# One product of the first batch on GpSimd, and a later load of w1, in a spectral filter followed by a low-rank mixer

## The chip, the cores and the metric

The kernel runs on one core of a Trainium2 chip. The metric is the device time of one execution in microseconds. Before the change the median of three runs is 516.92 us (514.62 to 517.74).

## What is computed

x has 8 batches of 3136 x 256 values in f32. Each batch goes through a real Fourier transform along the 3136, a multiplication by a complex filter per frequency and column, and the transform back. The result y then goes through a low-rank mixer along the 3136 and a two-layer network along the 256:

```
X = rfft(x, axis=1);  y = irfft(X * (filt_r + 1j * filt_i), n=3136, axis=1)
h = y.transpose(0, 2, 1) @ U @ V            # U: 3136 x 32, V: 32 x 3136
u = y + h.transpose(0, 2, 1)
out = u + relu(u @ w_ch1) @ w_ch2           # w_ch1: 256 x 1024, w_ch2: 1024 x 256
```

## The kernel before, in words

The transform of length 3136 is split as 49 x 64. For each batch `f1` or, for batches 0 and 1, `f1_turned` (L269) does the first stage on TensorE. `mid` (L319) does the middle: it goes over 12 pairs of frequency groups k = (1, 2), (3, 4) ... (23, 24) and the single group k = 0, which comes third. In this text pairs are counted from 0, so pair 9 is k = (19, 20); with k = 0 in the third place it is step i = 10 of the loop. For each step a first product `pz` on TensorE (L384), then a multiplication of `pz`, read from PSUM, with both parts of the filter `fab` on VectorE (L392), which gives `uv`; then, some steps later, `s3` (L334): a second product `pe` on TensorE (L345, in batch 0 two matmuls, and an unread one ahead of it that keeps TensorE busy), which ScalarE copies to `e3` (L355). How many steps later is set by the length that the list `todo` may have (L398).

The results are turned in DRAM. SyncE's queue stores `e3` in groups of two pairs to `ct` (L364; of the third group, pairs 8 and 9 together and pair 10 alone), and `load_e2` (L412) loads each group back, turned, as rows of `eb` (L416). Pair 11 of batch 0 goes straight to `eb` as four single rows, two on SyncE's queue and two on GpSimd's (L359). Instructions of one queue leave in order, so a store that stands behind a load back waits until that load's own stores have landed. `rank` (L419) multiplies `e3` with the transformed U (`uh`), which gives h; VectorE copies h to the first 32 rows of `eb` (L438). `s4` (L445) multiplies `eb` with `sv`, whose first 32 rows are V, reordered from `vnat` by `v_rows` (L200); its result is `ut`, that is u. `mm1` (L484) and `mm2` (L538) are the two layers, over groups of 512 rows.

For batches 1 to 7 a plan deals the steps of the other stages between the `mm1` and `mm2` of earlier rows. For batch 0 the order is written out by hand (L580 to L625), and that is where the change lies:

- GpSimd's queue issues the loads of the filters, V (`vnat`), `sv`, the first x of batch 1 and w1 (L593), then copies the third part of the filters to the upper 64 partitions in four copies (`spread_filters(2)`, L160), then reorders the first half of V (L595), and later issues its two rows of pair 11.
- The 13 steps of `mid` follow; after step 8 ScalarE copies `uh` out of PSUM (`u_copied`, L236, two copies), after step 10 the load back of group 0 is put into SyncE's queue. Then come a further part of `mid`, the load back of group 1, the first 20 matmuls of `rank`, the rest of `mid` with its loads back, the second half of V on VectorE, and the rest of `rank`.
- Then GpSimd reads a few values of `eb` into `seen` (L620), which makes it wait until the loads back have landed; behind that it issues the further x loads of batch 1 and the load of w2 (L623).

PSUM banks of `pz` come from a ring of four (`z`), those of `pe` in batch 0 from a ring of two (`o`). The pool tag `asb` has four buffers that batch 0 does not use.

Of the kernel before, what the change touches and what calls it, by code (L numbers as in the profile page):

```python
# [11 lines left out]
F32 = mybir.dt.float32  # L12
# [4 lines left out]
NQ, NR = 49, 64  # L17
# [13 lines left out]
def row_of(k1, part):  # L31

    return 4 * (2 * ((k1 - 1) % 8) + part) + (k1 - 1) // 8
# [47 lines left out]
def kernel(  # L81
# [11 lines left out]
    nc = tc.nc  # L93
# [15 lines left out]
    sb = ctx.enter_context(tc.tile_pool(name="sb", bufs=1))  # L109
    ps = ctx.enter_context(tc.tile_pool(name="ps", bufs=2, space=bass.MemoryType.PSUM))  # L110

    def bank(tag, name, dtype=F32):

        return ps.tile([128, 512 if dtype == F32 else 1024], dtype, tag=tag, bufs=4 if tag == "z" else 2, name=name)

    def dram(t, off, dims):
        return bass.AP(tensor=t, offset=off, ap=[list(d) for d in dims])

    def view(t, off, dims):
        return bass.AP(tensor=t.tensor, offset=t.offset + off, ap=[[t.ap[0][0], t.shape[0]]] + [list(d) for d in dims])  # L120
# [39 lines left out]
    def spread_filters(i):  # L160
        s = slice(PARTS[i], PARTS[i + 1])
        copies = ((nc.vector.tensor_copy, nc.scalar.copy), (nc.vector.tensor_copy, nc.scalar.copy),
                  (nc.gpsimd.tensor_copy, nc.gpsimd.tensor_copy))[i]

        for s in (slice(PARTS[2], 19), slice(19, NK)) if i == 2 else (s,):
            for f, copy in enumerate(copies):
                copy(fab[64:128, f, s, :], fab[0:64, f, s, :])
# [12 lines left out]
    w1sb = cst.tile([128, 2, NH], F16)  # L180
# [19 lines left out]
    def v_rows(copy, a, z):  # L200
        copy(sv[0:RANK, a:z], vnat.rearrange("p (q r) -> p r q", r=NR)[:, a:z])
# [60 lines left out]
    def unread(p, n, size=512):  # L262
        for _ in range(n):
            nc.tensor.matmul(p[:, 512 - size:512], m64[:, 0:128], m64[:, 0:size], start=True, stop=True, skip_group_check=True)
# [29 lines left out]
    def turn(b, g):  # L294
        if g == 3:
            t = a20[b]
            pt = bank("z" if b else "o", "pt", F16)
            for dh in range(2):
                nc.tensor.transpose(pt[0:64, 128 * dh:128 * dh + 128], t1[b][1][:, dh, :], idn)
            nc.scalar.copy(t[0:64], pt[0:64, 0:DM])  # L300
            return t
        t = sb.tile([128, 8, DM], F16, tag="a2", bufs=3, name="a2")
        for half in range(2):
            pt = bank("m" if b == 0 and g == 1 and half == 0 else "z", "pt", F16)
            if b == g == half == 0:
                unread(pt.bitcast(F32), 2)
            for i in range(4):
                for dh in range(2):
                    nc.tensor.transpose(pt[:, 256 * i + 128 * dh:256 * i + 128 * dh + 128],
                                        t1[b][0][:, dh, 8 * g + 4 * half + i, :], idn)  # L310
            (nc.scalar.copy if half or (g and b == 0) else nc.vector.tensor_copy)(  # L311
                t[:, 4 * half:4 * half + 4, :].rearrange("p k d -> p (k d)"), pt)
        return t
# [5 lines left out]
    def mid(b, tag="z"):  # L319
        a2 = {}  # L320

        def load_a2(g):
            if b < 2:
                a2[g] = turn(b, g)
                return
            if g == 3:
                t = a20[b % 2]
                nc.sync.dma_start(t[0:64], ct0[b].ap())
            else:
                t = sb.tile([128, 8, DM], F16, tag="a2", bufs=3, name="a2")  # L330
                nc.sync.dma_start(t, dram(ct1[b], 8 * g * DM, [[24 * DM, 128], [1, 8 * DM]]))
            a2[g] = t

        def s3(ks, uv, o):  # L334
            n = len(ks) * DM
            i = (ks[0] - 1) // 2
            pe = bank(tag, "pe")

            direct = b == 0 and ks[0] > 22
            ms = (gmp, gsmp) if direct or not ks[0] else (gm, gsm)  # L340
            if b == 0 and ks[0] > 8:

                unread(pe, 1)
            for f, w in enumerate(ms if b == 0 else ms[:1]):
                nc.tensor.matmul(pe[:, 0:n], w, uv[:, f, o:o + n], start=(f == 0), stop=(b > 0 or f == 1))  # L345
            if not ks[0]:
                e3[b, 6] = sb.tile([128, DM], F16, tag="e30", bufs=2, name="e30")
                nc.scalar.copy(e3[b, 6], pe[:, 0:n])

                nc.sync.dma_start(eb[96:97, :, :], e3[b, 6][0:64])  # L350
                return
            if i % 2 == 0:
                e3[b, i // 2] = sb.tile([128, 4, DM], F16, tag="e3", bufs=6, name="e3")
            t = e3[b, i // 2]
            nc.scalar.copy(t[:, 2 * (i % 2):2 * (i % 2) + 2, :].rearrange("p k d -> p (k d)"), pe)  # L355
            if direct:
                for n, k in enumerate(ks):
                    for part in range(2):
                        (nc.sync if part else nc.gpsimd).dma_start(  # L359
                            eb[32 + row_of(k, part):33 + row_of(k, part), :, :],  # L360
                            t[64 * part:64 * part + 64, 2 * (i % 2) + n, :])
            elif i % 2 or b == 0 and i == 10:
                n = 4 if i % 2 else 2
                nc.sync.dma_start(dram(ct2[b][i // 4], 2 * (i % 4 // 2 * 2) * 128 * DM, [[DM, 128], [128 * DM, n], [1, DM]]), t[:, 0:n, :])  # L364

        if b == 0:
            spread_filters(0)
        for g in (0, 3, 1, 2) if b > 1 else (0, 3):
            load_a2(g)
        todo = []  # L370
        first_at = 2 if b < 2 else 6
        for i, ks in enumerate(PAIRS[:first_at] + [(0,)] + PAIRS[first_at:]):
            n = len(ks) * DM
            if b == 0 and i == 1:
                spread_filters(1)
            if b < 2 and i in (3, 7):
                load_a2(i // 4 + 1)
            pz = bank("z", "pz")
            if b == i == 0:
                unread(pz, 2)  # L380
            if ks[0]:
                src = a2[(ks[0] - 1) // 8]
                k = (ks[0] - 1) % 8
                nc.tensor.matmul(pz, a2m, src[:, k:k + 2, :].rearrange("p k d -> p (k d)"), start=True, stop=True)  # L384
            else:
                nc.tensor.matmul(pz[:, 0:n], a20m, a2[3], start=True, stop=True)
            o = 512 if ks[0] % 4 == 3 else 0
            if o == 0:
                uv = sb.tile([128, 2, 1024], F16, tag="uv", bufs=4, name="uv")
            zin = bass.AP(tensor=pz.tensor, offset=pz.offset, ap=[[pz.ap[0][0], 128], [0, 2], [1, n]])  # L390
            fin = view(fab[:, 0, ks[0], 0:1], 0, [[NK * DM, 2], [1, n]])
            nc.vector.tensor_mul(uv[:, :, o:o + n], zin, fin)  # L392
            todo.append((ks, uv, o))
            if b and (o or not ks[0]):

                nc.vector.tensor_sub(uv[0:64, 0, 0:o + n], uv[0:64, 0, 0:o + n], uv[64:128, 1, 0:o + n])  # L396
                nc.vector.tensor_add(uv[64:128, 0, 0:o + n], uv[64:128, 0, 0:o + n], uv[0:64, 1, 0:o + n])  # L397
            if len(todo) > (3 if b else 2):  # L398
                s3(*todo.pop(0))
            yield  # L400
        for n, it in enumerate(todo):
            s3(*it)
            if b or n == 0:
                yield
        if b == 0:
            load_e2(0, 2, [0])
            for part in range(3):
                load_e2(0, part, [1])
        yield


    def load_e2(b, part, hs=(0, 1)):  # L412

        n = 12 if (b, part) == (0, 2) else 16
        for h in hs:
            nc.sync.dma_start(eb[32 + part:32 + 4 * n:4, 32 * h:32 * h + 32, :].rearrange("p (q r) d -> p q (r d)", r=8),  # L416
                              dram(ct2[b][part], 8 * h * DM, [[NR * DM, n], [16 * DM, 4], [1, 8 * DM]]))
# [172 lines left out]
        next(f1s[0])  # L590
    nc.gpsimd.dma_start(sv[32:97], sv_d.rearrange("k (r q) -> k r q", q=NQ))
    load_x(1, 0)
    nc.gpsimd.dma_start(w1sb, moe_w_ch1.rearrange("(h dd) c -> dd h c", h=2))  # L593
    spread_filters(2)
    v_rows(nc.gpsimd.tensor_copy, 0, 32)  # L595
    for i in range(13):
        next(mids[0])
        if i == 8:
            u_copied(put)
        if i == 10:  # L600
            load_e2(0, 0, [0])
    next(mids[0])
    load_e2(0, 1, [0])
    next(ranks[0])
    next(mids[0])
    v_rows(nc.vector.tensor_copy, 32, NR)
    next(ranks[0])
    for _ in ranks[0]:
        pass
# [21 lines left out]
    for b in range(1, NB):  # L631
        a, z = S[b - 1], S[b]
# [57 lines left out]
```

## Time and profile before

| | us |
|---|---|
| median of three runs | 516.92 |
| the profiled execution | 516.43 |
| its span | 514.6 |
| TensorE busy | 490.5 (95%) |
| ScalarE busy | 377.1 (73%) |
| VectorE busy | 366.2 (71%) |
| GpSimd busy | 80.6 (16%) |

The time of the profiled execution is 1.8 us over its span; the span runs from the first to the last instruction that is shown. In the stretches from 108 us on TensorE is busy throughout (58.00 of 58.00 us in each of the next three stretches of one batch's length). In the first 60 us it is not: 7.12 of the first 15.00, 12.88 of the next, then 10.39 and 12.24. The head up to about 60 us is therefore the part in which waits decide. A line of the timeline gives start, duration of the group, engine, line, operation, what is written and read, how many instructions are merged, and in square brackets the idle time before and what ended it. PEclk is the granted clock of TensorE, 1.00 being full.

### The profile page before, as it was taken

To read this page: it belongs to the slowest core of one execution; us is meant where nothing else is said; L and a number is where in the kernel's file an instruction comes from. 1 tells how busy PE (TensorE), PEld (TensorE's weight loads), DVE (VectorE), ACT (ScalarE), POOL (GpSimd) and SP (SyncE) were. 2 spreads that over 40 slices of the span, in tenths; PEclk is the share of its full clock that TensorE was granted. 3 is DMA by queue.
4 is the path that set the end of the run, shared out by engine and by line. 5 is a ranking of instruction groups with operands and counts; after the bars stand their busy time and mean duration, and the time that the engine had idled before them with its cause. 6 is when DMAs were issued, how large, how long until landed. Compare 5 with 4: busy or idle time off the path is not lost.

```text
span 514.6 us, 11909 instructions
## 1 busy us (share of the span) xinstructions
PE 490.5 (95%) x4754; PEld 349.6 (68%) x4754; DVE 366.2 (71%) x497; ACT 377.1 (73%) x704; POOL 80.6 (16%) x122
## 2 busy tenths in 40 slices
PE   3887899999999999999999999999999998999996
PEld 3645566776767777777767777777677765676665
DVE  5886599579847986679747986679846997853332
ACT  6874778867986689667986689667886676666663
POOL 6662010002001110002001110002001000011110
PEclk9998999999999999999999999999999999999999
DMA  8987926957877286837877286837877136644454
GB/s 187 175 206 174 181 74 172 281 171 176 216 229 251 69 186 190 298 130 177 213 227 254 69 185 202 262 156 184 218 228 240 65 126 206 212 153 149 126 162 163
DMA packets 76016, 94.52 MB, mean 184 GB/s; under 512 B 5795, under 2 KB 58979, under 8 KB 75960
## 3 DMA queue, kind: packets, MB, share of 16 engines
q1 hardware_dynamic: 61256, 52.17, 33.9%
q0 software_dynamic: 14704, 41.58, 31.4%
q8 instruction: 37, 0.61, 0.5%
q14 instruction: 19, 0.16, 0.1%
HBM read 58.35 MB, written 50.92 MB: 212 GB/s over the span
## 4 chain that ended last, share of the span: by engine, by line
PE 81%; DVE 8%; DMA 4%; issue 1%; ACT 1%; SPq 0%; POOL 0%; DVEq 0%; POOLq 0%
PE pc L544 31%; PE phh L488 30%; DVE uv L392 5%; PE pu L456 5%; PE pf L250 4%; PE pe L345 4%; PE pz L384 3%; PE pc L536 3%; DMA w2sb<-in_moe_w_ch_dram 2%; PE ph L423 1%; DVE uv L397 1%; DMA eb<-ct 1%; DVE uv L396 1%; DMA ct<-e 1%; DVE och L556 1%
## 5 line engine op out<-in xcount | busy, mean ns | idle before, releaser
L491 ACT ACTIVATE h<-phh 128x512 f16<-128x512 f32 x392 | 235.9, 603 | 83.2 <-PE phh L488 81.7
L544 PE MATMUL pc<-w2sb,h 128*128 128x256 f16 x1568 | 233.7, 272 | 1.2 <-DMA w2sb<-in_moe_w_ch_dram 1.2
L488 PE MATMUL phh<-ut,w1sb 128*128 128x512 f16 (+7 forms) x896 | 233.3, 352 | 0.4 <-DVE ut L463 0.4
L544 PEld LDWEIGHTS <-h 128*128 128x128 f16 x1568 | 151.7, 97 | 91.8 <-issue 1.5
L392 DVE TENSOR_TENSOR uv<-pz,fab 128x1024 f16<-128x1024 f32 (+1 forms) x104 | 120.6, 1177 | 12.5 <-PE pz L384 10.5
L561 POOL DMA_DIRECT2D out_dram<-och x48 | 39.1, 814 | 402.0 <-DVE och L556 318.8
L488 PEld LDWEIGHTS <-w1sb 128*128 128x128 f16 x896 | 78.9, 97 | 19.8 <-issue 1.5
L556 DVE COPY och<-pc 128x512 f32<-128x512 f32 x74 | 51.0, 689 | 44.4 <-PE pc L536 43.5
L355 ACT CAST e<-pe 128x512 f16<-128x512 f32 x96 | 56.6, 591 | 21.0 <-PE pe L345 20.2
L463 DVE CAST ut<-pu 128x392 f16<-128x392 f32 x92 | 48.5, 557 | 17.9 <-PE pu L456 16.0
L255 ACT CAST asb<-pf 98x512 f16<-98x512 f32 x96 | 57.3, 599 | 0.2
L438 DVE COPY eb<-h 32x4096 f16<-32x4096 f16 x32 | 38.2, 1232 | 14.2 <-ACT h L435 14.2
L552 DVE TENSOR_TENSOR och<-pc,tur 128x512 f32<-128x512 f32 x24 | 16.5, 689 | 39.8 <-PE pc L544 37.3
L345 PE MATMUL pe<-uv,m 128*128 128x512 f16 (+1 forms) x117 | 41.3, 371 | 3.6 <-DVE uv L392 1.5
L456 PE MATMUL pu<-sv,eb 97*128 97x49 f16 x1024 | 40.5, 187 | 3.3 <-DMA eb<-ct 3.1
L456 PEld LDWEIGHTS <-eb 97*128 97x128 f16 x1024 | 37.7, 98 | 4.8 <-DVE eb L438 3.4
L536 PE MATMUL pc<-idn,ut 128*128 128x128 f16 (+1 forms) x302 | 40.8, 219 | 0.0
L384 PE MATMUL pz<-a,m 128*128 128x512 f16 x96 | 36.2, 379 | 1.1 <-DVE a L311 1.0
L250 PE MATMUL pf<-x,ws 98*98 98x256 f16 x192 | 36.6, 273 | 0.0
L396 DVE TENSOR_TENSOR uv<-uv 64x1024 f16<-64x1024 f16 (+1 forms) x49 | 30.9, 630 | 1.7
L536 PEld LDWEIGHTS <-ut 128*128 128x128 f16 (+1 forms) x302 | 28.8, 98 | 3.9 <-issue 0.6
L397 DVE TENSOR_TENSOR uv<-uv 64x1024 f16<-64x1024 f16 (+1 forms) x49 | 30.7, 627 | 0.7
(80 smaller groups left out, 264.9 us busy)
## 6 DMA issues: line engine op xcount, KB each, us to landing
out_dram<-och POOLq DMA_DIRECT2D x48, 512.0 KB, 4.4
ct<-e SPq DMA_DIRECT2D x47, 256.0 KB
eb<-ct SPq DMA_DIRECT2D x46, 256.0 KB
x<-in_x_dram POOLq DMA_DIRECT2D x28, 392.0 KB, 7.8
ct<-asb SPq DMA_DIRECT2D x24, 384.0 KB
a<-ct SPq DMA_DIRECT2D x18, 512.0 KB
tu<-tu SPq DMA_DIRECT2D x48, 64.0 KB
tur<-tu SPq DMA_DIRECT2D x12, 256.0 KB
```

Of the source, the lines that this page charges most:

```text
L250: nc.tensor.matmul(pf[0:98, 256 * s:256 * s + 256], ws[:, (8 * c + j) * 98:(8 * c + j + 1) * 98], t[:, j, :], start=(s == 0), stop=True, s ...
L255: nc.scalar.copy(dst, src)
L345: nc.tensor.matmul(pe[:, 0:n], w, uv[:, f, o:o + n], start=(f == 0), stop=(b > 0 or f == 1))
L355: nc.scalar.copy(t[:, 2 * (i % 2):2 * (i % 2) + 2, :].rearrange("p k d -> p (k d)"), pe)
L384: nc.tensor.matmul(pz, a2m, src[:, k:k + 2, :].rearrange("p k d -> p (k d)"), start=True, stop=True)
L392: nc.vector.tensor_mul(uv[:, :, o:o + n], zin, fin)
L456: nc.tensor.matmul(pu[:, NQ * i:NQ * i + NQ], eb[:, 8 * n + i, d], sv[:, 8 * g + i, :], start=(i == 0), stop=True, skip_group_check=True)
L488: nc.tensor.matmul(ph[:, o:o + n], w1sb[:, dh, 128 * t:128 * t + 128], utv(b)[:, dh, t0:t0 + n], start=(dh == 0), stop=(dh == 1), skip_gro ...
L491: nc.scalar.activation(h, ph, RELU)
L536: nc.tensor.matmul(d, w, idn, start=False, stop=(dh == 1), skip_group_check=True)
L544: nc.tensor.matmul(o, gr.h[tt][:, 128 * i:128 * i + 128], w2sb[:, tt, :], start=(tt == 0), stop=(tt == 7 and turned(gr)), skip_group_check ...
L556: nc.vector.tensor_copy(gr.och[:, i - 1:i + 1, :], gr.pc.rearrange("p (j d) -> p j d", d=DM))
```

## The change

In batch 0, pair 9 is multiplied by GpSimd in place of VectorE. GpSimd does not read PSUM, so ScalarE copies `pz` to an f32 tile `zf` first. The list `todo` may hold three steps in batch 0 too, so each second product of batch 0 comes one step later than before. The load of w1 is issued on GpSimd's queue behind that multiplication. `u_copied` moves from step 8 to step 10. Both halves of V are reordered by VectorE, after the products. SyncE's instructions keep their places in the program, but since stores come one step later, the order of its queue is now: stores of group 0 and of pairs 4 and 5, load back of group 0, store of pairs 6 and 7, store of pairs 8 and 9, load back of group 1, store of pair 10, the two rows of pair 11, the other loads back. Before, the store of pairs 6 and 7 stood ahead of the load back of group 0, and the store of pair 10 ahead of the load back of group 1. On TensorE the first 20 matmuls of `rank` now come ahead of the second product of pair 10, where they came behind it.

```diff
+            by_pool = (b, i) == (0, 10)
+            if by_pool:
+
+                zf = sb.tile([128, 512], F32, tag="asb", bufs=4, name="zf")
+                nc.scalar.copy(zf, pz)
+            z = zf if by_pool else pz
+            zin = bass.AP(tensor=z.tensor, offset=z.offset, ap=[[z.ap[0][0], 128], [0, 2], [1, n]])
             fin = view(fab[:, 0, ks[0], 0:1], 0, [[NK * DM, 2], [1, n]])
-            nc.vector.tensor_mul(uv[:, :, o:o + n], zin, fin)
+            (nc.gpsimd if by_pool else nc.vector).tensor_mul(uv[:, :, o:o + n], zin, fin)
             todo.append((ks, uv, o))
...
-            if len(todo) > (3 if b else 2):
+            if len(todo) > 3:
                 s3(*todo.pop(0))
...
     load_x(1, 0)
-    nc.gpsimd.dma_start(w1sb, moe_w_ch1.rearrange("(h dd) c -> dd h c", h=2))
     spread_filters(2)
-    v_rows(nc.gpsimd.tensor_copy, 0, 32)
     for i in range(13):
         next(mids[0])
-        if i == 8:
+        if i == 10:
             u_copied(put)
-        if i == 10:
+            nc.gpsimd.dma_start(w1sb, moe_w_ch1.rearrange("(h dd) c -> dd h c", h=2))
             load_e2(0, 0, [0])
...
-    v_rows(nc.vector.tensor_copy, 32, NR)
+    for h in range(2):
+        v_rows(nc.vector.tensor_copy, 32 * h, 32 * h + 32)
```

More of the change, by code (lines that the diff above doesn't have):

```diff
@@ L389, in mid @@
                 uv = sb.tile([128, 2, 1024], F16, tag="uv", bufs=4, name="uv")
-            zin = bass.AP(tensor=pz.tensor, offset=pz.offset, ap=[[pz.ap[0][0], 128], [0, 2], [1, n]])
+            by_pool = (b, i) == (0, 10)
[4 more added lines that the diff above has]
+            zin = bass.AP(tensor=z.tensor, offset=z.offset, ap=[[z.ap[0][0], 128], [0, 2], [1, n]])
             fin = view(fab[:, 0, ks[0], 0:1], 0, [[NK * DM, 2], [1, n]])
-            nc.vector.tensor_mul(uv[:, :, o:o + n], zin, fin)
+            (nc.gpsimd if by_pool else nc.vector).tensor_mul(uv[:, :, o:o + n], zin, fin)
             todo.append((ks, uv, o))
```

## The prediction, made before the result was known

> **What bounds the kernel now.** I read the page's busy shares first: TensorE is busy 95% of the 514.6 us span, and after 108 us every slice shows it full, so nothing that the change touches can shorten the steady part. What is left is the head, where the change lies. The chain of work that ended last, in order of time, says what holds the head (start, us, what):
>
> ```profile
> 32.13 2.35 DVE uv L392 x2
> ...
> 36.57 0.37 ACT e L355
> 36.94 3.57 DMA ct<-e
> ...
> 42.77 4.31 DMA eb<-ct
> ...
> 48.87 10.53 DMA w2sb<-in_moe_w_ch_dram
> 59.41 0.04 issue
> 59.45 0.60 PE pc L544 x4
> ```
>
> The reader is to see that the chain leaves the multiplications at about 36 us and from there is a chain of transfers: the last store of batch 0's products (ct), the loads back (eb), GpSimd's look at them, the x loads and w2 behind that look, and TensorE waits for w2. After 59.45 us it is work. So the price of the change is how far it moves the store issued at 36.94 us and the loads behind it. The timeline of SyncE's queue shows why the store left then:
>
> ```profile
> 27.87 5.02 SPq L364 DMA_DIRECT2D ct<-e  x3
> 35.61 0.59 SPq L416 DMA_DIRECT2D eb<-ct  x1
> 36.31 1.07 SPq L364 DMA_DIRECT2D ct<-e  x2
> 37.47 0.53 SPq L416 DMA_DIRECT2D eb<-ct  x1
> ...
> 40.57 2.99 SPq L416 DMA_DIRECT2D eb<-ct  x4
> ```
>
> The first load back needs both stores of group 0. They were issued at 25.61 and 27.87, yet the queue sits from 32.9 to 35.6 until they have landed; the two stores behind it go at 36.31 and 36.94, although their data (ScalarE's copies of pairs 9 and 10) were there at 34.6 and 35.75. The timelines of VectorE and of GpSimd:
>
> ```profile
> 22.48 13.13 DVE L392 TENSOR_TENSOR uv<-pz,fab 128x1024 f16<-128x1024 f32 x12
> 35.53 1.48 DVE L201 COPY sv<-vnat 32x1568 f16<-32x1568 f16 x1
> 38.67 4.62 DVE L438 COPY eb<-h 32x4096 f16<-32x4096 f16 x4 [1.66 <-ACT h L435]
> ```
> ```profile
> 21.07 0.76 POOL L593 DMA_DIRECT2D w1sb<-in_moe_w_ch_dram  x1
> ...
> 26.53 4.28 POOL L167 COPY fab<-fab 64x1536 f16<-64x1536 f16 x3 [0.89 <-DMA fab<-in_filt_i_dram]
> 30.87 2.90 POOL L201 COPY sv<-vnat 32x1568 f16<-32x1568 f16 x1
> 37.45 1.08 POOL L359 DMA_DIRECT2D eb<-e  x2 [3.68 <-ACT e L355]
> ```
>
> VectorE has no gap from 22.48 to 35.53: twelve products at a pitch of 1.13 us. GpSimd is free from 33.8 to 37.45. Last, busy time by stretches (PE, PEld, DVE, ACT, POOL, clock, DMA share, GB/s):
>
> ```profile
> 30.00:32.00 2.00, 1.84 (x10) 0.79 (x9) 2.00 (x2) 2.00 (x6) 1.94 (x2) 1.00 1.01 214
> 32.00:34.00 2.00, 1.89 (x9) 0.76 (x8) 2.00 (x3) 1.09 (x2) 1.77 (x1) 1.00 1.02 280
> 34.00:36.00 2.00, 1.68 (x25) 0.71 (x24) 2.00 (x3) 1.17 (x2) 0.00 (x0) 1.00 0.55 164
> 36.00:38.00 2.00, 1.08 (x9) 0.36 (x8) 1.01 (x1) 0.96 (x2) 0.55 (x2) 1.00 0.50 110
> 38.00:40.00 2.00, 2.00 (x23) 1.38 (x23) 1.33 (x2) 1.73 (x8) 0.53 (x1) 1.00 1.09 292
> ```
>
> The DMA engines are full until w1 lands (21.07 + 13.3 = 34.4 us), then half empty for 4 us.
>
> **The change, part by part.** Pairs are counted 0 to 11; pair 9 (k 19, 20) is the one that moves.
>
> *VectorE.* It loses pair 9's product: pairs 10 and 11 move up one place, to 32.13 and 33.27, and VectorE is done at 34.40, 1.13 us earlier. Both halves of V follow, 2 x 1.48, to 37.4. Before, h came at 38.27 + 0.37 = 38.64; so V stays hidden with over 1 us of cover, and GpSimd's 2.90 us copy was off the chain too. V: 0.
>
> *ScalarE.* It gains the copy of pair 9 to f32. The same shape (128x512 from PSUM, L355) takes 0.59 us, about 0.5 of it pitch. The queue of products is one longer, so each second product stands one product later on TensorE, and ScalarE's copies with it. I walk it with the pitches of the trace (product to next product on TensorE 0.87 us; a-copies 1.81 for two; u copies 0.82): pair 5's copy at 30.7, the f32 copy 31.15 to 31.74, pair 6 at 31.65, the two u copies 32.12 to 32.94, pair 7 to 33.53 (before: 32.5), pair 8 to 34.0.
>
> *GpSimd.* Its four filter copies end at 30.8; it waits for the f32 copy and starts at 31.8. No GpSimd product is in the trace. Lower bound: the one-input copy L167, 1.46 us for 1536 elements, 0.95 ns each, gives 0.97 us for 1024; two inputs cannot be quicker than one. Upper: the strided copy L201, 1.85 ns each, once for each of two inputs, 3.8 us. I take 1.95, the plain copy once for each of two inputs, since the rows here lie side by side: done at 33.75. The Trainium skill (GPSIMD Engine Reference, Performance versus the Vector engine) gives 4497 ns for 2048 f32 elements of a two-input operation, held to one read port: by it an estimate of 2.25 us, done 0.3 later, and the sum below would be unchanged. VectorE's pitch stays 1.13 beside the filter copies, so I charge no mutual blocking.
>
> *TensorE.* Second product of pair 9: ScalarE must first empty a bank (pair 7's copy, 33.53) and GpSimd be done (33.75): 33.8 to 34.4, copied by 35.0 (before 34.6). Then the first part of the rank product comes, which before stood behind pair 10's second product and now stands ahead of it, and reads pair 9: it ends at 35.25. Pair 10: 35.4 to 36.0, copied by 36.6 (before 35.75, so 0.85 later). Pair 11: copied by 37.3 (before 37.16). VectorE's 1.13 us is thus spent in TensorE's order; h moves by 0.1.
>
> *SyncE.* New order: store of pairs 4-5, load back of group 0, store of pairs 6-7, store of pairs 8-9, load back of group 1, store of pair 10, two single-row moves, load back of group 2. With w1 away from 21 to 34, the full stretch ends earlier by w1's 512 KB at 214 GB/s, 2.4 us, so the first load back goes at about 33.2 in place of 35.6. But the store of pairs 6-7 now goes only at 33.85 (pair 7's copy, 33.53, and the queue), and the load back of group 1 needs it landed. Landing takes 3.57 by the chain's row: 37.4. In front of that wait stands nothing; behind it stands the store of pair 10, ready at 36.6: issued at 38.05 after the load's 0.59. That is 1.1 later than 36.94. Bounds: with a landing under 2.2 us (33.85 + 2.2 + 0.59) pair 10's data would set it, at 36.65, so -0.3; with 4.9, the longest that the trace allows for this store (32.5 to 37.4), +2.4. I take +1.1, by the row of the same kind of store.
>
> *w1.* GpSimd issues it at 33.75, 0.76 long, ahead of its two single-row moves at 37.3, which it does not delay. It is first needed at 50.3. Its 2.4 us of transfer fall where the stores and loads of the chain go. The stretches 34 to 38 have about 1.9 us free, then 38 to 40 is full: 0.5 is left over; I take +0.4, bounds 0 and +2.4. The Trainium skill (DMA: Bandwidth & Descriptors, Issuing engines are not separate DMA queues) says that transfers of all issuing engines interleave on the same 16 engines; group 0's second store, issued at 27.87 beside w1 and not landed before 34.7, agrees, and by the rule alone the price would be the whole 2.4 (rival 2).
>
> *TensorE's clock.* TensorE waits from 41.2 to 44.28 for the loads back, and the clock granted afterwards is 0.81, 0.50 and 0.84 in the stretches 44 to 50. A longer wait can lengthen that: from nothing to 16 tiles at the slow pitch of 0.43 us in place of 0.26, 2.7 us in all, of which about 1.4 is paid already (44.28 to 49.7 for 4.2 us of work). I take 0, because the chain runs past it through the x loads and w2, for which TensorE stands still 1.2 us; upper end +0.1.
>
> *Sum.* +1.1 + 0.4 = +1.5 us on the loads back, hence on GpSimd's look, the x loads and w2. The profiled execution took 516.43 us, 0.5 below the median of the runs; it would become 517.9, and the median 518.4.
>
> **Rivals.**
> 1. *The wait taken out of SyncE's queue wins.* With the DMA engines emptier, stores land in about 2.2 us; the store of pair 10 goes at 36.65 and lands sooner by up to 1.3 us (3.57 - 2.2). For it: the stretches after w1 are half empty. Against it: w1 is in them now, and 3.57 was measured in them without it. Change: -0.3 to -1.6, so 515.3 to 516.6.
> 2. *w1 collides in full.* The whole 2.4 us and the longer landing of the pair 6-7 store: +1.1 + 2.4, up to +4.8, about 521. For it: 38 to 40 us is full already. Against it: the gaps before.
> 3. *GpSimd's product is slow, and the end lands on the slow side.* TensorE's second products of pairs 9, 10 and 11 stand in order behind it. Pair 10 overtakes the SyncE wait when the product takes over 3.4 us, and each us beyond is one on the chain. A loss of 1% (5.2 us) needs about 7.1 us (3.4 + 5.2 - 1.5). For it: no row. Against it: 3.8 is the upper bound by the rows. 523 or more.
> 4. *The change does nothing that can be seen*: the w2 wait of 1.2 us swallows it. For it: TensorE could go on. Against it: w2 moves with the loads back. About 517.
>
> **How the numbers follow.** Likeliest, +0.5 to +2.5: 0.43. Rival 1: 0.20, rival 4: 0.07, rival 2: 0.18. Rival 3 or a collision that adds to it, past 1%: 0.08; faster by over 1%, for which no row has room: 0.04. A measurement of this kernel can tell about 1% from no change (the runs of before lie 3 us apart), so all but the last two lie within it, except 0.03 of rival 2's upper end. Faster 0.04, same 0.85 (0.43 + 0.20 + 0.07 + 0.15), slower 0.11. Range: from rival 1's lower end, 515.2, to most of rival 2, 521.2 (+4.3); outside lie the two last cases and what is left of rival 2, and the scatter of the runs at the ends. The likeliest case alone is 517.4 to 519.4, and 518.4 is its sum.
>
> **What would show it.** Right: twelve minus one VectorE products ending near 34.4; the GpSimd product near 31.8, about 2 us; first load back near 33; pair 10's store at about 38, behind a load back that waited for a store; w2 landing some 1.5 us later than 59.4. Wrong: pair 10's store before 37 (rival 1); loads back that take well over 4.3 us (rival 2); a GpSimd product over 3.4 us (rival 3); a w1 that lands after 50 and stalls the first w1 product, which I exclude.

## The result: 1.0% slower, and the profile after

| | before | after |
|---|---|---|
| median of 8 runs, us | 516.01 (514.38 to 518.97) | 520.62 (519.65 to 523.95) |
| the profiled execution | 516.43 | 520.59 |
| its span | 514.6 | 518.8 |

The ratio is 1.0102, with a 95% interval of 1.0078 to 1.0125. The forecast was +1.5 us, no change that a measurement can tell; the change costs 4.6 us at the medians and 4.16 between the two profiled executions. The time lies in the forecast range, near its upper end. One execution of all those below, the profiled one of e1, took 852.85 us at a granted clock of 0.56 and counts in no time given here.

The chain of waits of the changed kernel (start, us, what) has the same links as before from the store (`ct<-e`) on:

```profile
31.17 2.14 POOL uv L398
...
36.34 0.59 ACT e L355
...
37.26 7.29 DMA ct<-e
...
46.81 4.20 DMA eb<-ct
...
52.81 10.28 DMA w2sb<-in_moe_w_ch_dram
63.09 0.04 issue
63.13 0.60 PE pc L550 x4
```

Ahead of the store the view goes back over ScalarE's copy of pair 11 (36.34) to GpSimd's product (31.17), but pair 10's store waits for neither: its own copy, pair 10's, runs from 35.69 to 36.28, and SyncE's queue comes to it only at 37.26, behind a load back issued at 36.68.

Held against the chain of before: the last store leaves 0.32 us later (37.26 for 36.94) and takes 3.72 us longer to land (7.29 for 3.57). The loads back are 0.11 quicker and w2 0.25 quicker; the work between them is the same to 0.01. That gives +3.68 at TensorE's first product with w2 (63.09 for 59.41). The stores of the output, lined up against those of before, stay +3.69 until 329 us; from 337 us on they are at +4.15, behind one wait for a load back in batch 5, which adds 0.46. 3.69 + 0.46 = 4.15 of the 4.16 us. So in this pair of profiles the loss is the landing of one store. The profile of before is a late one, though: in the five other profiles below that have w1 early and the old order, pair 10's store leaves at 35.5 to 36.2 and not at 36.94.

The timeline of SyncE's queue (start, duration of the group, queue, line, operation, written<-read, instructions merged):

```profile
28.84 2.09 SPq L364 DMA_DIRECT2D ct<-e  x2
32.42 0.59 SPq L422 DMA_DIRECT2D eb<-ct  x1
33.11 1.84 SPq L364 DMA_DIRECT2D ct<-e  x2
36.68 0.53 SPq L422 DMA_DIRECT2D eb<-ct  x1
37.26 0.81 SPq L364 DMA_DIRECT2D ct<-e  x1
...
44.61 2.99 SPq L422 DMA_DIRECT2D eb<-ct  x4
```

The first load back goes 3.19 us sooner than before (32.42 for 35.61). Before, it waits for group 0's two stores, which leave while w1 is being loaded, the second at 27.87 and the first here:

```profile
25.61 0.38 SPq L364 DMA_DIRECT2D ct<-e  x1
```

By the updates of their semaphores (the counters that tell of a landing) in the trace, the first lands at 34.66 and the second at 35.53, that is 9.1 and 7.7 us after their issue. In the changed kernel the two leave at 25.18 and 28.84 and take 5.1 and 3.5.

There the store of pairs 6 and 7 goes right behind the first load back, and the load back of group 1 then waits from that store's issue at 33.11 until 36.68; pair 10's store stands behind it. The timelines of VectorE and GpSimd:

```profile
22.05 12.00 DVE L398 TENSOR_TENSOR uv<-pz,fab 128x1024 f16<-128x1024 f32 x11
33.97 2.92 DVE L201 COPY sv<-vnat 32x1568 f16<-32x1568 f16 x2
```
```profile
31.17 2.13 POOL L398 TENSOR_TENSOR uv<-zf,fab 128x1024 f16<-128x1024 f32 x1 [1.47 <-issue]
33.24 0.78 POOL L604 DMA_DIRECT2D w1sb<-in_moe_w_ch_dram  x1
37.22 1.12 POOL L359 DMA_DIRECT2D eb<-e  x2 [3.19 <-ACT e L355]
```

VectorE ends its products at 34.05, 1.56 us sooner, V takes 2.92 and is done at 36.9, before h comes (38.4). GpSimd's product is done at 33.3. Pair 10's store waits for none of this; w1's load, issued at 33.24, is beside it. Busy time by stretches (PE, PEld, DVE, ACT, POOL, clock, DMA share, GB/s):

```profile
32.00:34.00 2.00, 1.53 (x12) 0.43 (x14) 2.00 (x3) 1.32 (x5) 2.00 (x2) 1.00 0.33 68
34.00:36.00 2.00, 1.98 (x26) 0.91 (x18) 2.00 (x3) 0.87 (x2) 0.03 (x1) 1.00 1.02 246
36.00:38.00 2.00, 1.15 (x12) 0.63 (x11) 0.88 (x1) 1.24 (x3) 0.78 (x2) 1.00 0.45 61
38.00:40.00 2.00, 2.00 (x24) 1.26 (x21) 1.55 (x2) 1.96 (x9) 0.34 (x1) 1.00 0.90 169
40.00:42.00 2.00, 0.96 (x6) 0.29 (x3) 2.00 (x3) 0.20 (x2) 0.00 (x0) 1.00 1.07 268
42.00:44.00 2.00, 0.00 (x0) 0.00 (x0) 1.06 (x1) 0.00 (x0) 0.00 (x0) 1.00 0.51 156
```

The stretch 36 to 38 is the one to look at: three transfers are outstanding on SyncE's queue (store of pairs 8 and 9 from 34.59, load of group 1 from 36.68, pair 10's store from 37.26) and w1 on GpSimd's, yet the DMA share is 0.45 and 61 GB/s move. The trace's packet records, added up by queue, say whose bytes they are (KB begun in each microsecond, rounded down):

| us | before: SyncE | before: GpSimd | after: SyncE | after: GpSimd |
|---|---|---|---|---|
| 35 | 74 | 0 | 258 | 14 |
| 36 | 22 | 0 | 10 | 22 |
| 37 | 192 | 0 | 1 | 86 |
| 38 | 284 | 4 | 6 | 106 |
| 39 | 256 | 26 | 94 | 124 |
| 40 | 149 | 32 | 167 | 78 |
| 41 | 69 | 2 | 154 | 108 |
| 42 | 116 | 0 | 126 | 36 |
| 43 | 304 | 0 | 141 | 2 |

From 36 to 39 SyncE's queue moves 18 KB in the changed kernel and 499 KB before, while w1 begins on GpSimd's queue at 22 to 106 KB a microsecond. Then both share. The store of pairs 8 and 9 lands at 43.61, 9.0 us after its issue, and pair 10's at 44.55; w1 has landed at 43.1 (33.24 + 9.9). TensorE waits 7.3 us for the loads back (3.1 before), and its granted clock is 0.50 from 46 to 52.

### The profile page after: what moved, and what is told of

The parts are those of the page before. It is cut to its first block, busy times and chain, and to the rows that moved or that the text cites. A ratio compares the mean times of both kernels' runs of the same rounds, so it can differ in the third digit from the quotient of the medians.

```text
span 518.8 us, 11910 instructions
## 1 busy us (share of the span) xinstructions
PE 490.0 (94%) x4754; PEld 348.8 (67%) x4754; DVE 366.7 (71%) x497; ACT 377.5 (73%) x705; POOL 80.0 (15%) x122
## 4 chain that ended last, share of the span: by engine, by line
PE 78%; DMA 8%; DVE 7%; ACT 3%; POOL 2%; issue 2%; SPq 0%; DVEq 0%; POOLq 0%; ACTq 0%
PE pc L550 29%; PE phh L494 28%; PE pu L462 5%; PE pf L250 4%; PE pe L345 4%; DVE uv L398 3%; PE pz L384 3%; PE pc L542 3%; DMA ct<-e 3%; DMA w2sb<-in_moe_w_ch_dram 2%; DMA x<-in_x_dram 2%; DMA eb<-ct 2%; PE ph L429 1%; DVE uv L403 1%; DVE uv L402 1%
## 5 line engine op out<-in xcount | busy, mean ns | idle before, releaser
L384 PE MATMUL pz<-a,m 128*128 128x512 f16 x96 | 36.2, 379 | 2.8 <-DVE uv L398 1.2
```

## The experiments

Theory 1: the whole loss is w1, which now meets the stores (rival 2, larger than priced). Theory 2: the loss is the new order of SyncE's queue, in which pair 10's store stands behind a load that waits for another store; w1's place only decides where the wait is seen. A third possibility was GpSimd's product or the moved copies. Whole kernels come first, each timed beside the kernel before.

### Whole kernels: one part undone, or one part alone

**e1_w1_early**: the changed kernel with w1 back in its old place.

```diff
     load_x(1, 0)
+    nc.gpsimd.dma_start(w1sb, moe_w_ch1.rearrange("(h dd) c -> dd h c", h=2))
     spread_filters(2)
...
             u_copied(put)
-            nc.gpsimd.dma_start(w1sb, moe_w_ch1.rearrange("(h dd) c -> dd h c", h=2))
```

> The changed kernel with the load of w1 alone put back to its old place, ahead of the filter copies. Theory 1 (late w1 collides with the last stores of batch 0): the store of pair 10 lands in about 3.6 us in place of 7.3. But w1 then delays the first stores as before, and in the new order of SyncE's queue each load back stands ahead of a store: store of pair 10 issued at about 38 to 40, so 0 to 3 us over the kernel before, and less than the 4.6 us of the changed kernel. Theory 2 (the cost is the order of SyncE's queue and the longer list, not w1): the time stays at about 4.6 us over before.

Measured: 519.26 at the middle of five runs against 515.84, ratio 1.0067 (1.0042 to 1.0093). Its only trace is of the execution that took 852.85 us and is not read. Three quarters of the loss stay although w1 is where it was. Theory 1 falls as the whole story; the 4.6 us of theory 2 lie just inside the interval.

**e2_only_w1**: the kernel before, with only w1 moved to behind step 10.

```diff
     load_x(1, 0)
-    nc.gpsimd.dma_start(w1sb, moe_w_ch1.rearrange("(h dd) c -> dd h c", h=2))
...
         if i == 10:
+            nc.gpsimd.dma_start(w1sb, moe_w_ch1.rearrange("(h dd) c -> dd h c", h=2))
             load_e2(0, 0, [0])
```

> The kernel before with the load of w1 alone moved to behind step 10, so that it is issued at about 33.8 us behind GpSimd's copy of V; products, list and SyncE's order as before. Theory 1: the two last stores, issued at 36 to 37, meet w1's packets; they land in about 7 us in place of 3.6, and the time is 3 to 4 us over before. Theory 2: no loss; with the DMA engines free earlier, 0 to 1 us under before.

Measured: 516.52, ratio 1.0022 (1.0002 to 1.0041). In its profile pair 10's store is issued at 35.37, 1.57 us sooner than before, and lands at 41.5, 6.1 us later: the longer landing is there, and sooner stores pay for most of it. At 0.7 us over before it is far from theory 1's 3 to 4, and a little over theory 2's none.

**e3_w1_behind_rows**: the changed kernel with w1 issued behind GpSimd's two rows of pair 11.

```diff
             u_copied(put)
-            nc.gpsimd.dma_start(w1sb, moe_w_ch1.rearrange("(h dd) c -> dd h c", h=2))
             load_e2(0, 0, [0])
...
     next(mids[0])
+    nc.gpsimd.dma_start(w1sb, moe_w_ch1.rearrange("(h dd) c -> dd h c", h=2))
     for h in range(2):
```

> The changed kernel with w1 issued still later, behind GpSimd's two single-row moves (about 38.3 us). Theory 1: the store of pair 10 (issued at about 37.3) runs ahead of w1's packets, which come some 2.5 us after their issue, and lands in about 4 us, at about 41.3; w1 then meets the loads back and costs them 0.5 to 2.5. Time between 0.5 and 3.5 us over before. Theory 2: 4.6 us over before as in the changed kernel.

Measured: 518.2, ratio 1.0041 (1.002 to 1.0063), so about half of the loss goes. Pair 10's store lands in 4.1 us (37.12 to the loads back at 41.29). Now the loads back meet w1: the packet records have SyncE's queue at 50, 2 and 0 KB in the microseconds from 40, 41 and 42, and GpSimd's at 60, 156 and 194. The same pause has moved one link down the chain.

**e4_old_order**: the changed kernel with w1 late, but the old order of SyncE's queue and of the rank product.

```diff
-            if b or n == 0:
+            if b or n < 2:
                 yield
...
             nc.gpsimd.dma_start(w1sb, moe_w_ch1.rearrange("(h dd) c -> dd h c", h=2))
+        if i == 11:
             load_e2(0, 0, [0])
     next(mids[0])
+    next(mids[0])
     load_e2(0, 1, [0])
```

> The changed kernel with the loads back of groups 0 and 1 put one step later, so that SyncE's queue and TensorE's rank product have the order of the kernel before; w1 stays late. Theory 1: the store of pair 10 is issued near 36, but lands in about 7 us all the same: 2.5 to 4 us over before. Theory 2: the loss is gone, within 0.5 us of before or up to 1 us under.

Measured: 520.63 (517.13 to 521.16), ratio 1.0084 (1.0055 to 1.0112), 4.8 us over before, for theory 1's 2.5 to 4 and theory 2's none. The old order alone brings nothing back in the whole kernel. Its profiled execution is the quickest of the six, 517.13, with a head only 0.69 us later than before, though pair 10's store takes 6.75 us to land (35.39 to 42.14). What the other five do is in no trace. Both e2 and e4 have the late w1 and the old order; they differ in the rest of the change alone, and by 4.1 us (1.4 to 4.8 when the runs are resampled). w1's issue, behind step 10 in both, comes at 32.06 in e2's profile and at 33.40 in e4's. So beside a late w1 the rest of the change is not free, and which part of it costs no run shows.

### The head by itself

The whole kernels scatter by 3 to 4 us. The next kernels cut the program behind the first two groups of 512 rows; the later batches, their groups and their outputs are left out. In h_before the program is that of the whole kernel up to about 67 us, where the first layer of the second group ends.

```diff
-    for n, gr in enumerate(groups):
+    for n, gr in enumerate(groups[:2]):
...
-        mm2(groups[-1], t)
+        mm2(groups[1], t)
```

**h_before**, **h_after**: the two kernels with this cut. **h_w1_early**: e1's edit with it. **h_only_w1**: e2's.

> Head alone of the kernel before: only the first two of the 49 row groups go through the two layers, the rest of the work (later batches, their groups and their outputs) is left out; up to 63 us the instructions are those of the whole kernel. It ends at about 85 us. It is the base for the other head kernels.

> Head alone of the changed kernel (the same work left out). Theory 1: the whole loss arises in the head, at the landing of pair 10's store: 3.7 us over the head of before in most runs, as in the profile (w2 landed 63.09 against 59.41). Theory 3 (part of the loss is a stall in a later batch that the shift makes likelier): the head gives clearly less than the 4.6 us of the whole kernel, 3 or under.

> Head alone with every part of the change but w1's move (the same work left out). Theory 1 with SyncE's order as a second term: the first load back waits for stores that w1 delays, and the stores behind it with it: 1.5 to 3 us over the head of before, the 3.5 us of the whole kernel less what arises later. If w1's place were all, 0 to 0.5.

> Head alone of the kernel before with w1's move alone (the same work left out). In the profile of the whole kernel the last store was issued 1.6 us sooner and landed in 6.1 us, so that the two nearly cancel: 0 to 0.7 us over the head of before. If late w1 alone cost the loss: 3 to 4.

Then **h_old_order** (e4's edit), **h_old_early** (e4's edit and e1's: only GpSimd's product, the longer list, the u copies and V's reorder remain of the change), **h_w1_rows** (e3's edit), and **h_dve_early** (e1's edit, and VectorE multiplies all pairs):

```diff
-            by_pool = (b, i) == (0, 10)
+            by_pool = False
```

> Head alone (two row groups, the rest left out) of the changed kernel with the order of SyncE's queue and of the rank product as before; w1 stays late, GpSimd keeps its product. If the new order costs 3.4 us beside late w1 (store group 2 landed 44.86 against 41.45 in the two heads with late w1), this one stands where w1's move alone stands: 2.0 us over the head of before, and 4 us under the head of the changed kernel. If GpSimd's product or the longer list is the cost, it stays near the changed kernel, 5 to 6 over.

> The same with w1 at its old place too, so that of the change only GpSimd's product with its f32 copy, the longer list, the u copies and V on VectorE remain (the rest of the work left out). If order and w1 are the whole loss: within 0.7 us of the head of before. If GpSimd's product costs: 1 us or more over.

> Head of the changed kernel with w1 issued behind the two single-row moves (the rest of the work left out). The store of pair 10 is issued at about 37.4 as in the changed kernel, but lands in about 4.1 us, as in that kernel's whole profile: group 2 loads back some 3.3 us sooner than in the changed kernel's head. 2.5 to 3.5 us over the head of before; if w1 then holds the loads back, up to 4.5.

> Head with the new order and w1 early, and pair 9 multiplied by VectorE from PSUM again (no f32 copy; the rest of the work left out). The store of pair 10 waits for the load back of group 1, which waits for the store of pairs 6 and 7, not for a product: 4.2 us over the head of before, as with GpSimd's product. If GpSimd's product is the cost: 2 us or more less.

Last **h_half**: h_old_order with half of w1 early.

```diff
+    nc.gpsimd.dma_start(w1sb[:, :, 0:512], moe_w_ch1.rearrange("(h dd) c -> dd h c", h=2)[:, :, 0:512])
     spread_filters(2)
...
-            nc.gpsimd.dma_start(w1sb, moe_w_ch1.rearrange("(h dd) c -> dd h c", h=2))
+            nc.gpsimd.dma_start(w1sb[:, :, 512:], moe_w_ch1.rearrange("(h dd) c -> dd h c", h=2)[:, :, 512:])
```

> Head alone (two row groups, the rest left out) of the changed kernel with the old order, and w1 split by columns: the first half loaded early, the second half late, behind GpSimd's product. With all of w1 late this head took 87.08 us, with all early 83.73. If late w1 costs by its bytes: about 85.4. If any late transfer on GpSimd's queue holds up the stores: near 87. If the stores only lose when w1's tail meets them: under 84.3.

Medians in us. The heads were timed in three groups, beside which the kernel before took 515.72, 515.62 and 515.86. "Landed" is when SyncE's queue goes on with the loads that wait for pair 10's store.

| head | order | w1 | median (lowest to highest) | pair 10's store | landed |
|---|---|---|---|---|---|
| h_before | old | early | 83.78 (82.3 to 85.47) | 35.55 | 39.02 |
| h_old_early | old | early | 83.73 (82.65 to 85.4) | 35.78 | 39.28 |
| h_half | old | half, half | 85.61 (84.03 to 88.08) | 35.94 | 42.04 |
| h_only_w1 | old | late | 85.82 (84.51 to 86.98) | 35.40 | 41.51 |
| h_old_order | old | late | 87.08 (86.73 to 87.31) | 34.78 | 42.28 |
| h_w1_rows | new | later | 87.24 (85.22 to 87.83) | 37.40 | 40.82 |
| h_w1_early | new | early | 88.01 (86.87 to 88.79) | 40.47 | 43.99 |
| h_dve_early | new | early | 88.16 (87.85 to 88.57) | 39.50 | 43.02 |
| h_after | new | late | 89.73 (88.39 to 90.14) | 37.58 | 44.92 |

Four heads lost more than was expected of them: h_after 5.95 us over h_before (3.7 expected), h_w1_early 4.23 (1.5 to 3), h_only_w1 2.04 (0 to 0.7) and h_old_order 3.30 (2.0). The others came as one of their cases had it.

Four of these heads are a square in which the rest of the change is the same:

| | w1 early | w1 late | w1's step |
|---|---|---|---|
| old order | 83.73 | 87.08 | +3.35 |
| new order | 88.01 | 89.73 | +1.72 |
| the order's step | +4.28 | +2.65 | both: +6.00 |

Both theories hold, each for a part, and the parts overlap by 4.28 + 3.35 - 6.00 = 1.63 us. The sizes are rough. From the runs within 1.5% of their head's quickest alone, w1's steps are +3.68 and +1.32, the order's +4.36 and +2.00, both +5.68, the overlap 2.36; when all runs are resampled, 95% of the overlaps lie between 0 and 2.8 us. Each step by itself stays clear of zero. The timeline of SyncE's queue in h_w1_early shows the order's part without w1's:

```profile
35.59 0.60 SPq L422 DMA_DIRECT2D eb<-ct  x1
36.29 1.08 SPq L364 DMA_DIRECT2D ct<-e  x2
39.87 0.55 SPq L422 DMA_DIRECT2D eb<-ct  x1
40.47 0.76 SPq L364 DMA_DIRECT2D ct<-e  x1
...
43.99 2.98 SPq L422 DMA_DIRECT2D eb<-ct  x4
```

The store of pairs 6 and 7 goes at 36.29, behind the first load; the second load waits 3.58 us for it, and pair 10's store goes at 40.47, with a landing of 3.5 as before. Its data were there at 36.54 (ScalarE's copy, 35.95 + 0.59), so it is the queue that holds the store, and not the new place of `rank` on TensorE, which the "new order" also has in it. In h_old_order it is the other way round:

```profile
32.92 0.60 SPq L422 DMA_DIRECT2D eb<-ct  x1
34.14 1.41 SPq L364 DMA_DIRECT2D ct<-e  x2
...
42.28 2.96 SPq L422 DMA_DIRECT2D eb<-ct  x4
```

Nothing waits in the queue, pair 10's store (the second of the two at 34.14) goes at 34.78, and its landing takes 7.4 us. In h_after a late w1 lets the first load go 3 us sooner than in h_w1_early (32.64 for 35.59) and with it pair 10's store (37.58 for 40.47), and then w1 doubles the landing behind it (7.3 for 3.5).

The other heads: h_old_early equals h_before (-0.05), so beside an early w1 the rest of the change costs and gains nothing that these runs can show. Beside a late one it costs 1.26 (h_old_order over h_only_w1), which stays unexplained. h_dve_early equals h_w1_early (+0.15), so GpSimd's product does not matter there. Half of w1 costs about half (+1.9 of +3.35), with a scatter of 4 us that makes it no more than a hint; in its profile pair 10's store takes 6.0 us to land, no less than with all of w1 in e2 and h_only_w1 (6.1 and 6.05). h_w1_rows has the store back to 3.4 us and still loses 3.5: GpSimd's look at the first half of the loads comes only at 46.22, because the loads meet w1, issued at 39.45.

### Whole kernels made from this

**f_old_early**: the changed kernel with w1 early and the old order (the edits of e1 and e4 together). **f_loads_first**: the kernel before, with the loads back of the second halves of groups 0 and 1 ahead of both of group 2.

```diff
         if b == 0:
-            load_e2(0, 2, [0])
-            for part in range(3):
+            for part in range(2):
                 load_e2(0, part, [1])
+            load_e2(0, 2)
```

**f_both**: both edits together.

> Whole kernel: of the change only GpSimd's product with its f32 copy, the longer list, the u copies and V on VectorE; the order of SyncE's queue and of the rank product and w1's place are those of before. Its head alone took 83.73 us against 83.78. If nothing outside the head matters: within 0.7 us of the kernel before. If what remains costs in later batches (the e4 kernel lost 4.3 us where its head lost 3.3): 1 to 2.5 us over.

> The kernel before with one change: the second-half loads back of groups 0 and 1 are issued ahead of both loads of group 2, into the 1.2 us in which SyncE's queue waits for the store of pair 10 (39.3 to 40.5 us). If the last load back sets the x loads and w2 as the chain says: the last one is issued about 1.2 us sooner, head 1 us shorter, whole kernel 0.5 to 1 us under before. If the DMA engines, not the queue, set its landing: no difference.

> f_old_early with the same order of the loads back: 0.5 to 1 us under before, like f_loads_first, if GpSimd's product is worth nothing; up to 1.5 under if the 1.1 us that VectorE saves reaches the store of pair 10 once the queue is free.

Measured, beside 515.86 of the kernel before: f_old_early 516.08, ratio 1.0002 (0.9979 to 1.0024); f_loads_first 515.69, 0.9992 (0.9973 to 1.0011); f_both 516.07, 1.0002 (0.9975 to 1.0029). With the old order and the early w1 the whole loss is gone, so in the whole kernel too it takes the late w1 or the new order to bring it. The whole kernels make the same square: 516.08 with neither, 519.26 with the order alone (e1), 520.63 with the late w1 alone (e4), 520.62 with both. There the order alone costs 3.18, the late w1 alone 4.55 and both together 4.54, so the two parts overlap more than in the heads, by 3.19; resampled, 95% of these overlaps lie between -0.4 and 4.2. No version beats the kernel before by more than its scatter, and the 0.5 to 1 us expected of f_loads_first and f_both do not show. f_loads_first has its last load back and w2 sooner (w2 issued at 47.90 for 48.87), but the first half later, and TensorE waits longer for that.

The head does not say all of a whole run. f_old_early's profiled execution, its slowest of twelve (518.97), is 1.68 us ahead of before at the end of the head, and then TensorE waits in batch 5 for a load back (waits of TensorE between 240 and 470 us: engine, line, releaser, us in total, times, longest):

```profile
PE pu L462 <- DMA eb<-ct: 2.4, 1, 2.4
PE pe L345 <- DVE uv L403: 1.3, 1, 1.3
```

With what follows from it that costs 4.17 us. The first line is absent in before, in e4, f_loads_first and f_both; it is 0.3 in after, 1.3 in e2 and 2.1 in e3 (there 3.83 us in all). It comes and goes in kernels that share that code. That looks like scatter of up to 4 us, enough to hide a head's gain in any one profile, but no kernel has two profiles to show it.

## Why the prediction was wrong, step by step

- **VectorE and V: right.** Eleven products end at 34.05 (forecast 34.40) and V is done at 36.9 with h at 38.4.
- **ScalarE's copy and GpSimd's product: right.** The copy starts at 30.44 (31.15), the product at 31.17 (31.8) and takes 2.13 us (1.95, bounds 0.97 and 3.8). The estimate from the Trainium skill (GPSIMD Engine Reference, Performance versus the Vector engine), 2.25, is the nearer one. Rival 3 is out, and h_dve_early shows that the step has no price in the head with the new order and an early w1.
- **TensorE's order: right.** Second products of pairs 9, 10 and 11 start at 33.35, 35.06 and 35.71, the first part of the rank product between the first two, and pair 10's copy starts at 35.69.
- **SyncE's order: the mechanism was right, and the size came out for a reason that was half seen.** First load 32.42 (33.2), store of pairs 6 and 7 at 33.11 (33.85), load of group 1 at 36.68 (37.45), pair 10's store at 37.26 (38.05). The landing that was assumed for pairs 6 and 7, 3.57, is what the queue shows to the hundredth (33.11 to 36.68). That exactness is luck: the row it came from is of a store of 128 KB, and the store of pairs 6 and 7 has 256 KB. All is 0.74 to 0.79 early because w1's leaving frees 3.19 us ahead of the first load and not 2.4; e2, where only w1 moves, has that load at 32.67. So the term is +0.3 in place of +1.1 against the profile of before, and +1.0 to +1.7 against the five other profiles with an early w1 and the old order. It is this small only because w1 is gone: with w1 early the same order costs 4.28 in the head.
- **w1: the step that failed.** "The stretches 34 to 38 have about 1.9 us free, then 38 to 40 is full: 0.5 is left over; I take +0.4, bounds 0 and +2.4." Measured: +3.72 on one landing, 1.3 beyond the upper bound. The step took idle DMA share for room that w1's bytes could fill, and 2.4 us of bytes for the most that they can cost. The runs show that the stores lose their turn, not only their share: for one to three microseconds SyncE's queue hardly moves. In the changed kernel the engines are less than half busy meanwhile (0.45 in the stretch 36 to 38); in h_only_w1, where SyncE's queue begins 0 KB in the microseconds from 36, 37 and 38, GpSimd's transfers fill them for two of the three (shares 0.40, 1.01, 1.12). So empty engines are not what goes with the pause; w1 is. The trace of before had the sign of it, and the prediction, which quotes it, priced w1 by its bytes all the same: group 0's stores, issued at 25.61 and 27.87 while w1 was in flight, took 9.1 and 7.7 us to land.
- **The landing of pair 10's store: not repriced.** The sum let 3.57 stand for a store that left beside w1. The seven profiles with w1 near it have 6.0 to 7.4 (after, e2, e4, h_only_w1, h_old_order, h_half, h_after); e3, with w1 issued 0.75 us behind it, has 4.1; without w1 near it it is 3.3 to 3.6.
- **The clock: right that it does not set the end.** It falls to 0.50 for longer, and w2 is still waited for (0.5 us, 1.2 before).
- **The rivals.** Rival 2, w1 colliding in full, was given 0.18, with "about 521" at its end; it comes nearest. But it agrees in the sum more than in the mechanism: it put the longer landing on the store of pairs 6 and 7, which took 3.57 as in the main case, and its sign, loads back that take well over 4.3 us, did not come (4.20). It is the stores of pairs 8 to 10 that w1 held. Its reason against, "the gaps before", is the one that failed. Rival 1's sign, pair 10's store before 37, did not come either (37.26), and rival 4 is out.

Open: why a whole kernel loses 4.6 where its head loses 6.0, and e1 3.4 where its head loses 4.2; and why beside a late w1 the rest of the change costs 1.3 in the head and 4.1 in the whole kernel. TensorE is not full between 60 and 80 us (18.93 of 20 us before, 18.70 after), so a part can be taken up there; that is argued, not shown. e4, which loses 4.8 whole and 3.3 in its head, goes against it and is not explained.

## What to carry to other kernels

Half-empty DMA engines are no room for a transfer as long as another queue has something due on the chain: look at which stores and loads start in the first 3 to 4 us of the moved transfer, and price it by the longest landing that the trace shows for such a store beside such a transfer (here 9.1 and 7.7 us, in the trace of before), not by bytes over bandwidth. Before a producer is let come one step later, write out the in-order queue behind it: a store that falls behind a load which waits for another store can be held for that store's whole landing (3.58 us in h_w1_early). Two such changes are to be tried each alone and together, since here their costs do not add up.

## What the runs showed of the hardware that was not expected

- Transfers of SyncE's queue that are due when the late w1's bytes begin on GpSimd's queue almost stop for one to three microseconds: 18 KB in the three from 36 in the changed kernel, 0 KB in the three from 36 in h_only_w1 and in the two from 34 in e2. e3 shows it for loads back (2 KB in the two microseconds from 41). Landings of pair 10's store go from 3.3 to 3.6 us up to 6.0 to 7.4. The two rows of pair 11 on GpSimd's queue do not do it: before, SyncE's queue moves 284 and 256 KB in the microseconds from 38 and 39, beside 4 and 26.
- Beside an early w1 the first store's bytes begin late too: 1.9 to 3.4 us after its issue in the eight profiles that have it, 1.0 to 1.2 in the nine others (h_half, with half of w1 early, among them; e1 is not read).
- The Trainium skill (DMA: Bandwidth & Descriptors, Queues, rings and completion order) says that each DMA engine takes turns between the queues that have work, a packet at a time. An even turn does not show in these microseconds (40 packets begin on SyncE's queue and 107 on GpSimd's in the three from 36 in the changed kernel), and what holds SyncE's queue back there no run here shows.
- GpSimd's product of 1024 f32 by f16 elements a partition takes 2.13 us, 2.08 ns an element, beside VectorE's 1.09 for the same shape (12.00 us for eleven), GpSimd reading its f32 from SBUF and VectorE from PSUM.
